# Token-number scatters, first weight loads and two start-up stores in another order (attention, routed experts and a feed-forward layer in one kernel)

## The chip, the cores and the metric

The kernel runs on one core of a Trainium2 chip. The metric is the device time of one execution in microseconds (us). PE is the matmul engine (TensorE) and PEld its weight loads, DVE is VectorE, ACT is ScalarE, POOL is GpSimd, SP is SyncE. SPq, ACTq and POOLq are the instruction queues of those engines as far as they issue transfers (DMAs).

## What is computed

Three layers follow one another. The attention layer pools keys and values by eight, the second layer sends each token to one of eight experts, and the third is a plain feed-forward layer.

```python
k_p = k.reshape(B, H, Sp, 8, D).mean(axis=3)          # q, k, v: (8, 8, 576, 64)
v_p = v.reshape(B, H, Sp, 8, D).mean(axis=3)
attn = softmax(scale * q @ k_p.T)
x = (attn @ v_p) as (4608, 512)                       # one row per token

logits = normed(x) @ normed(expert_emb).T / tau       # 8 experts
expert_idx = argmax(logits); gate_w = softmax(logits)[expert_idx]
for e in range(8):
    h = relu(x[mask_e] @ w1[e])                       # 512 -> 1024
    out[mask_e] = gate_w[mask_e] * (h @ w2[e])        # 1024 -> 512

h = x @ w_in                                          # 512 -> 2048
return (h * clip(h + 3, 0, 6) / 6) @ w_out            # 2048 -> 512
```

## The kernel before

The order of the instructions is written out by hand (a manual schedule): on every engine and queue they run in the order in which the program emits them, and each waits for what it reads or overwrites.

**Phase 1, attention and routing, 36 tiles of 128 tokens.** The loop at line 852 runs over t = 0 to 37. In step t it emits `emit_S(t)` (scores on PE, row maximum and subtraction on DVE), `emit_T(t-1)` (transposes on PE, copy on ACT), the exponential on ACT, the jobs that `todo[t]` holds, `emit_P(t-2)` (attention times values on PE, normalisation on DVE, a store of the tile's rows to `x_dram` from the ACT queue), the jobs of `late[t]`, and at the end of the step at most one entry of the list `prep`. A batch is 4.5 tiles. Its loads (`load_kv`, `load_q`) go out on the SP queue, and its pooling runs on POOL and partly on DVE (`pool_v`, `pool_k0`, `pool_k`; for the first two batches `half_v` and `head_k`). Two buffers of pooled keys, `kps[0]` and `kps[1]`, take turns; both are zeroed on POOL at the start (line 341).

**Routing.** The tiles form six groups of 7, 7, 6, 6, 5 and 5. When a group is through, a generator `emit_route` is put in a list, and `fill` emits a small DVE operation of it at a time between the operations of the tiles. Its last step (lines 571 to 574) writes the token numbers on POOL (`tok`) and then one `scatter` per tile: a tiny memset of `apart` and an indirect DMA of 128 rows of 64 bytes into the table `idx_dram`, each token's number at its place in its expert's list. The table is filled with a dummy number beforehand (lines 759 and 760), and one row of zeros is written behind the tokens of `x_dram` (line 761). Both are issued on the SP queue, the zeros read from `kps[1]`.

**Phase 2, experts, blocks of 256 tokens.** `emit_idx` reads token numbers from the table, `emit_gather` fetches the rows, `emit_wload` fetches a quarter of an expert's w1 or w2 (an indirect DMA from POOL, 512 KB), and `emit_wsplit` splits it into two parts (ACT and POOL or DVE) and emits the load of the same quarter of the next block. Four quarters j make a block: `emit_h(i, j)` needs the split of w1, `emit_y(i, j)` that of w2. In blocks 0 and 1 the w1 split runs on POOL, later on DVE. A block emits w1 splits two quarters ahead and calls `more()` three times per quarter; `more` empties the routing generators little by little. In block 1 at j = 2 all that is left of routing is flushed, and the token lists of the following blocks are asked for.

**The list `prep`** holds what phase 2 needs first: the token lists of three blocks (`ahead`), eight weight loads in one go, the gathers of blocks 0 and 1, the splits of w1 and w2 of quarter 0, the scaling of block 0's rows by their gates (`emit_gated(0)`) and the w1 split of quarter 1. One entry is taken per step from the step in which the expert counts of the first 20 tiles are there; from the third entry on, the gates of those tiles must have been emitted too. If entries are left at t = 36, they are emitted there, before the transposes of block 0 (`emit_xT(0)`).

**Phase 3**, the feed-forward layer, comes behind and isn't touched.

Of the kernel before, what the change touches and what calls it, by code (L numbers as in the profile page):

```python
# [21 lines left out]
def kernel(  # L22
# [27 lines left out]
    NJ = 4  # L50
# [280 lines left out]
    with ExitStack() as p1:  # L331
# [193 lines left out]
        def emit_route(t0, t1):  # L525
# [45 lines left out]
            tok = sm.tile([P, G, IW], I32, name="tok", bufs=2)  # L571
            nc.gpsimd.iota(tok, pattern=[[P, G], [0, IW]], base=P * t0, channel_multiplier=1)
            for t in range(t0, t1):
                scatter(idx_dram, pi[:, t - t0:t - t0 + 1], tok[:, t - t0, :], "ids")
            yield

        def emit_gate(t0, t1):
# [131 lines left out]

        gens = []  # L710

        gates = []
        gate_at = [0]
        calls = [0]
# [37 lines left out]
        for g in range(2):  # L752
# [3 lines left out]
        DR = 18  # L756
        dummy = one.tile([P, DR * IW], I32, name="dummy")
        nc.gpsimd.memset(dummy, NT)
        nc.sync.dma_start(out=idx_dram.rearrange("(p a b) o -> p a (b o)", p=P, b=DR),
                          in_=dummy.unsqueeze(1).to_broadcast([P, IDXN // P // DR, DR * IW]))  # L760
        nc.sync.dma_start(out=x_dram[NT:NT + 1, :], in_=kps[NKP - 1][0:1].rearrange("p h s c -> p (h s c)")[:, 0:XW])
        esq = xp.tile([P, DM], F32, name="sq")
        ess = one.tile([E, 1], F32, name="ess")
        nc.scalar.activation(out=esq[0:E], in_=emb_sb, func=AF.Square, accum_out=ess)
# [61 lines left out]
            at(2, head_k, 1, h, nc.gpsimd if h < HP - 1 else nc.vector, d=late)  # L826
        for g in range(2):
            at(2, half_v, 1, g, nc.gpsimd, d=late)
        at(5, emit_ve1, 1)
        at(6, emit_ve2, 1)  # L830
        for b in range(2, NB):
# [9 lines left out]
        gi = 0  # L841

        prep = [
            lambda: [ahead(i) for i in range(KA)],
            lambda: [emit_wload(w, g) for g in range(NJ) for w in ("w1", "w2")],
            lambda: (emit_gather(0), emit_gather(1)),
            lambda: emit_wsplit("w1", 0, nc.gpsimd),
            lambda: emit_wsplit("w2", 0, nc.gpsimd),
            lambda: emit_gated(0),
            lambda: emit_wsplit("w1", 1, nc.gpsimd),  # L850
        ]
        for t in range(NTILE + 2):
            if t == NTILE:

                while not PRE_U:
                    for g_ in gens + gates:
                        g_[1] = False
                    fill(100)
                if prep:
                    while gates:  # L860
                        for g_ in gens + gates:
                            g_[1] = False
                        fill(100)
                while prep:
                    prep.pop(0)()
                sc = sc_p
                PX[:] = [sc[:, g, :] for g in range(2)]
                emit_xT(0)
            exp = emit_S(t) if t < NTILE else lambda: None
            if 1 <= t <= NTILE:  # L870
                emit_T(t - 1)
            exp()
            for f, *a in todo.get(t, ()):
                f(*a)
            if t == NTILE + 1:
                pt = psA.tile([P, 2, 512], F32, name="pt")
                PY[:] = [pt[:, g, :] for g in range(2)]
                emit_h(0, 0)
            if 2 <= t:
                emit_P(t - 2)  # L880
            for g_ in gens + gates:
                g_[1] = False
            fill(2)
            for f, *a in late.get(t, ()):
                f(*a)
            if gi < len(GROUPS) and t - 2 >= GROUPS[gi][1] - 1:
                gens.append([emit_route(*GROUPS[gi]), False, GROUPS[gi]])
                gi += 1
            if PRE_U and prep and (len(prep) > 5 or not gates):
                prep.pop(0)()  # L890

# [70 lines left out]
    def more():  # L964
        for g_ in gens + gates:
            g_[1] = False
        fill(2)

    def block(i, first):
        key = CONV[i - 1] if 1 <= i <= len(CONV) else None  # L970
        for j in range(NJ):
            g = NJ * i + j
            if i == KA - 2 and j == 2:
                flush(gens)
                flush(gates)
                ahead(KA)
                ahead(KA + 1)
            if j == 0:
# [196 lines left out]
```

## Time and profile before

| | us |
|---|---|
| three runs | 1531.66, 1533.35, 1530.65 (median 1531.66) |
| the profiled execution, whole | 1527.47 |
| its span in the profile | 1525.8 |
| PE busy | 1456.0 (95%) |
| DVE, ACT, POOL busy | 780.3, 626.4, 514.5 |

A share of busy time is a mean over the three phases. Phase 1 takes the first 217 us or so (the transposes of block 0 begin at 217.00 us), the blocks 0 and 1 of phase 2 reach to some 280 us, and from 300 us on PE is busy nearly without a gap. The profiled execution stands 4.2 us under the median of the runs, and 1.7 us of it lie around the span.

### The profile page before, as it was taken

What the parts mean: (1) busy time and instruction counts of PE and PEld (TensorE: products, weight loads), DVE (VectorE), ACT (ScalarE), POOL (GpSimd) and SP (SyncE); (2) the same over time, 40 slices, a digit from 0 to 9 for tenths busy, and PEclk for the clock granted to TensorE, in tenths of its full rate; (3) what the DMA queues carried; (4) which work ended last, traced back from release to release, by engine and by line L of the source; (5) the groups of instructions that cost most, each with busy time, mean ns of one, the idle gap of its engine ahead of it and who ended that gap; (6) DMA issues with size and microseconds to landing.
All of it is one profiled execution on the core that took longest, in us unless ns stands there. A gap on an engine that the chain in (4) does not pass through costs nothing.

```text
span 1525.8 us, 22766 instructions
## 1 busy us (share of the span) xinstructions
PE 1456.0 (95%) x8874; PEld 1304.5 (85%) x8874; DVE 780.3 (51%) x1261; ACT 626.4 (41%) x986; POOL 514.5 (34%) x518
## 2 busy tenths in 40 slices
PE   5889788999999999999999999999999999999997
PEld 4888678899999999999788888888888888888886
DVE  5676646778777777666686322323232222323221
ACT  2545344556556566556343222222222222222221
POOL 3866568665665565545222000010101001010101
PEclk8889789999999999999999999999999999999999
DMA  9765432563862245252322010000101000010000
GB/s 297 259 229 163 163 98 76 169 200 81 266 200 58 75 120 160 72 159 41 113 97 72 0 42 16 29 28 1 56 0 57 1 29 28 5 51 1 28 0 28
DMA packets 88451, 136.15 MB, mean 89 GB/s; under 512 B 43369, under 2 KB 58409, under 8 KB 85874
## 3 DMA queue, kind: packets, MB, share of 16 engines
q1 hardware_dynamic: 45026, 69.10, 14.4%
q0 software_dynamic: 33488, 55.80, 12.2%
q10 hardware_dynamic: 9824, 9.73, 1.9%
q8 instruction: 72, 1.18, 0.3%
q14 instruction: 41, 0.34, 0.1%
HBM read 161.51 MB, written 33.33 MB: 128 GB/s over the span
## 4 chain that ended last, share of the span: by engine, by line
issue 37%; PE 12%; POOL 2%; POOLq 0%; ACT 0%
PE ph L1071 3%; PE psx L1089 3%; PE psy L1071 3%; PE psz L1089 3%; POOL out_dram L128 2%; POOL apart L127 0%; POOLq L1171 0%; POOLq L128 0%; ACT os L1099 0%
## 5 line engine op out<-in xcount | busy, mean ns | idle before, releaser
L157 POOL DMA_INDIRECT rw<-in_w_dram,wrow x179 | 220.1, 1230 | 181.5 <-DVE w1l L170 122.8
L128 POOL DMA_INDIRECT out_dram<-os,idc x36 | 35.1, 976 | 657.8 <-ACT os L1099 651.4
L1075 DVE SCALAR_TENSOR_TENSOR rg<-rg,ph 128x512 f32<-128x512 f32 x72 | 49.6, 689 | 206.9 <-ACT rg L1074 206.9
L1078 DVE TENSOR_TENSOR gl<-rg,gh 128x512 fp32r<-128x512 f32 x144 | 99.8, 693 | 100.7 <-ACT gh L1077 100.7
L1077 ACT ACTIVATE gh<-rg 128x512 fp32r<-128x512 f32 x144 | 91.2, 633 | 145.7 <-DVE rg L1075 144.0
L1075 DVE SCALAR_TENSOR_TENSOR rg<-rg,psy 128x512 f32<-128x512 f32 x72 | 49.5, 687 | 178.3 <-ACT rg L1074 178.3
L1074 ACT ACTIVATE rg<-ph,half 128x512 f32<-128x512 f32 x72 | 49.4, 686 | 208.7 <-PE ph L1071 208.7
L1074 ACT ACTIVATE rg<-psy,half 128x512 f32<-128x512 f32 x72 | 49.4, 686 | 198.7 <-PE psy L1071 198.7
L277 PE MATMUL psy<-hh,w2h 128*128 128x256 f32 x640 | 129.4, 283 | 0.0
L277 PE MATMUL psy<-hh,w2l 128*128 128x256 f32 x640 | 127.5, 280 | 0.0
L277 PE MATMUL psy<-hl,w2h 128*128 128x256 f32 x640 | 127.4, 280 | 0.0
L170 DVE TENSOR_TENSOR w1l<-rw,w1h 128x1024 fp32r<-128x1024 f32 x76 | 108.9, 1433 | 24.9 <-ACT w1h L169 14.9
L170 DVE TENSOR_TENSOR w2l<-rw,w2h 128x1024 fp32r<-128x1024 f32 x84 | 108.6, 1293 | 15.9 <-ACT w2h L169 11.8
L1089 PE MATMUL psx<-wol,gh 128*128 128x512 f32 x288 | 112.0, 389 | 0.0
L1089 PE MATMUL psz<-woh,gh 128*128 128x512 f32 x288 | 112.0, 389 | 0.0
L1089 PE MATMUL psx<-woh,gh 128*128 128x512 f32 x288 | 112.0, 389 | 0.0
L1089 PE MATMUL psx<-woh,gl 128*128 128x512 f32 x288 | 112.0, 389 | 0.0
L1089 PE MATMUL psz<-wol,gh 128*128 128x512 f32 x288 | 112.0, 389 | 0.0
L1089 PE MATMUL psz<-woh,gl 128*128 128x512 f32 x288 | 112.0, 389 | 0.0
L265 ACT ACTIVATE hh<-ph 128x512 fp32r<-128x512 f32 x78 | 46.6, 598 | 147.0 <-PE ph L262 135.9
L169 ACT ACTIVATE w2h<-rw 128x1024 fp32r<-128x1024 f32 x85 | 89.9, 1058 | 29.5 <-PE psy L277 18.5
L262 PE MATMUL ph<-xh,w1h 128*128 128x256 f32 x624 | 99.0, 280 | 1.5 <-ACT xh L248 1.5
(235 smaller groups left out, 3340.0 us busy)
## 6 DMA issues: line engine op xcount, KB each, us to landing
yT_dram<-ys SPq DMA_DIRECT2D x21, 512.0 KB
x_dram<-x ACTq DMA_DIRECT2D x36, 256.0 KB
raw<-in_w_in_dram SPq DMA_DIRECT2D x16, 512.0 KB
raw<-in_w_out_dram SPq DMA_DIRECT2D x16, 512.0 KB
yl<-yT_dram SPq DMA_DIRECT2D x8, 1024.0 KB
k_t<-in_k_dram SPq DMA_DIRECT2D x7, 1152.0 KB
q_t<-in_q_dram SPq DMA_DIRECT2D x7, 1152.0 KB
v_t<-in_v_dram SPq DMA_DIRECT2D x7, 1152.0 KB
```

The lines of the kernel that those rows point to most:

```text
L128: ins = nc.gpsimd.indirect_dma_start(out=dst, out_offset=bass.IndirectOffsetOnAxis(ap=idx, axis=0), in_=src, in_offset=None)
L157: nc.gpsimd.indirect_dma_start(out=RAW[nm][j], out_offset=None, in_=WROWS[nm], in_offset=bass.IndirectOffsetOnAxis(ap=wrow[:, i, j:j + 1], ...
L169: nc.scalar.activation(out=h, in_=r, func=AF.Copy)
L170: eng.tensor_tensor(out=l, in0=r, in1=h.bitcast(F32), op=ALU.subtract)
L262: nc.tensor.matmul(ph[:, f, :], lhsT=a[:, c, fs], rhs=b[:, c, :], start=(n == 0), stop=(n == 3 * KD - 1))
L277: nc.tensor.matmul(o, lhsT=a[:, f, P * c:P * c + P], rhs=b[:, f, :], start=(j == 0 and n == 0 and c % 2 == 0), stop=(j == NJ - 1 and n == ...
L1071: nc.tensor.matmul(ph, lhsT=a[:, c, :], rhs=b[:, c, :], start=(n == 0), stop=(n == 3 * KD - 1))
L1074: nc.scalar.activation(out=r, in_=ph, func=AF.Relu, scale=1.0 / 6.0, bias=half)
L1075: nc.vector.scalar_tensor_tensor(out=r, in0=r, scalar=1.0, in1=ph, op0=ALU.min, op1=ALU.mult)
L1077: nc.scalar.activation(out=gh, in_=r, func=AF.Copy)
L1078: nc.vector.tensor_tensor(out=gl, in0=r, in1=gh.bitcast(F32), op=ALU.subtract)
L1089: nc.tensor.matmul(PO[a], lhsT=x[:, ts], rhs=w, start=(f == 0 and n == 0), stop=(f == NF - 1 and n == 2))
```

## The change

- The scatters of a group are no longer emitted in one go: they go into a list `pend`, and `put(n)` emits n of them. A step of phase 1 that takes no entry of `prep` puts one, or two if more than seven wait. In phase 2 each `more()` puts one. All that wait are put before the first `ahead` and at the flush in block 1.
- `prep` has eight entries instead of seven: the eight weight loads of block 0 are spread over entries 2, 3, 5, 6, 7 and 8 (two, two, one, one, one, one), the gathers come fourth.
- The dummy fill of the table is emitted with the jobs of t = 3, behind the loads of batch 2 (t = 1); it stays on the SP queue.
- The row of zeros is issued on the ACT queue, at its old place in the program, where the first ACT operation of the kernel (square of the expert embeddings, line 764) now comes behind it.

```diff
-                scatter(idx_dram, pi[:, t - t0:t - t0 + 1], tok[:, t - t0, :], "ids")
+                pend.append(lambda t=t: scatter(idx_dram, pi[:, t - t0:t - t0 + 1], tok[:, t - t0, :], "ids"))
             yield
...
+        pend = []
+
+        def put(n=1):
+            while pend and n > 0:
+                n -= 1
+                pend.pop(0)()
...
-        nc.sync.dma_start(out=idx_dram.rearrange("(p a b) o -> p a (b o)", p=P, b=DR),
-                          in_=dummy.unsqueeze(1).to_broadcast([P, IDXN // P // DR, DR * IW]))
-        nc.sync.dma_start(out=x_dram[NT:NT + 1, :], in_=kps[NKP - 1][0:1].rearrange("p h s c -> p (h s c)")[:, 0:XW])
+
+        def fill_idx():
+            nc.sync.dma_start(out=idx_dram.rearrange("(p a b) o -> p a (b o)", p=P, b=DR),
+                              in_=dummy.unsqueeze(1).to_broadcast([P, IDXN // P // DR, DR * IW]))
+
+        nc.scalar.dma_start(out=x_dram[NT:NT + 1, :], in_=kps[NKP - 1][0:1].rearrange("p h s c -> p (h s c)")[:, 0:XW])
...
+        at(3, fill_idx)
...
-            lambda: [ahead(i) for i in range(KA)],
-            lambda: [emit_wload(w, g) for g in range(NJ) for w in ("w1", "w2")],
+            lambda: (put(99), [ahead(i) for i in range(KA)]),
+            lambda: (emit_wload("w1", 0), emit_wload("w2", 0)),
+            lambda: (emit_wload("w1", 1), emit_wload("w2", 1)),
             lambda: (emit_gather(0), emit_gather(1)),
-            lambda: emit_wsplit("w1", 0, nc.gpsimd),
-            lambda: emit_wsplit("w2", 0, nc.gpsimd),
-            lambda: emit_gated(0),
-            lambda: emit_wsplit("w1", 1, nc.gpsimd),
+            lambda: (emit_wsplit("w1", 0, nc.gpsimd), emit_wload("w1", 2)),
+            lambda: (emit_wsplit("w2", 0, nc.gpsimd), emit_wload("w2", 2)),
+            lambda: (emit_gated(0), emit_wload("w1", 3)),
+            lambda: (emit_wsplit("w1", 1, nc.gpsimd), emit_wload("w2", 3)),
         ]
...
             if PRE_U and prep and (len(prep) > 5 or not gates):
                 prep.pop(0)()
+            else:
+                put(1 + (len(pend) > 7))
...
         fill(2)
+        put()
...
                 flush(gates)
+                put(99)
                 ahead(KA)
```

## Rows read from the trace of the kernel before

**Rows 1.** Stretches: length, busy us and instructions of PE, PEld, DVE, ACT, POOL; clock, DMA.
```profile
7.00:217.00 210.00, 168.41 (x1175) 155.63 (x1176) 133.18 (x396) 94.94 (x207) 130.65 (x148) 0.85 0.65 211
217.00:300.00 83.00, 73.88 (x581) 70.76 (x580) 56.17 (x107) 40.43 (x60) 64.76 (x57) 0.96 0.32 96
300.00:990.00 690.00, 687.98 (x4806) 643.00 (x4805) 434.90 (x515) 344.37 (x491) 285.15 (x233) 1.00 0.35 103
```

**Rows 2.** Timeline, 13 to 41 us: start, duration, operation, [idle before it, its releaser].
```profile
13.84 14.53 SPq L761 DMA_DIRECT2D x_dram<-kp  x1
...
30.06 0.35 ACTq L491 DMA_DIRECT2D x_dram<-x  x1
...
35.25 0.51 DVE L789 TENSOR_TENSOR kp<-k_t 64x72 f32<-64x72 f32 x2 [4.35 <-DMA x_dram<-kp]
...
37.47 1.63 PE L434 MATMUL sc<-kp,q_t 128*64 128x144 f32 x10 [4.51 <-DVE ex L445]
...
40.71 1.22 PE L434 MATMUL sc<-kp,q_t 128*64 128x144 f32 x6 [1.61 <-POOL kp L789]
```

**Rows 3.** Timeline of the first 20 us.
```profile
3.99 1.09 POOL L341 MEMSET kp<- 128x576 f32 x2
...
6.08 0.46 DVE L785 TENSOR_TENSOR k_t<-k_t 128x288 f32<-128x288 f32 x1 [1.02 <-DMA k_t<-in_k_dram]
...
19.82 0.44 PE L394 MATMUL pm<-ident,vs 96*64 96x96 f32 x3 [2.01 <-POOL vs L780]
```

**Rows 4.** Timeline, 201 to 210 us: the fourth group's scatters.
```profile
201.52 1.01 POOL L128 DMA_INDIRECT idx_dram<-tok,pi  x1 [0.25 <-issue]
...
207.62 0.17 DVE L476 TENSOR_SCALAR rd<-px 128x8 f32<-128x8 f32 x1 [6.81 <-remote]
...
207.96 0.97 POOL L128 DMA_INDIRECT idx_dram<-tok,pi  x1 [0.21 <-issue]
...
209.17 3.26 PE L468 MATMUL px<-vp,eT 96*128 96x146 f32 x12 [5.35 <-DVE oh L543]
```

**Rows 5.** One stretch inside that series, columns as in Rows 1.
```profile
204.00:208.00 4.00, 0.00 (x0) 0.00 (x0) 0.38 (x4) 0.00 (x0) 3.22 (x7) 1.00 0.04 6
```

**Rows 6.** PE's waits, 0 to 226 us: us in total, times, longest.
```profile
PE pt L455 <- ACT ex L449: 5.1, 3, 2.4
```

**Rows 7.** Groups of instructions, 0 to 330 us: count, busy us, mean ns, idle before.
```profile
L157 POOL DMA_INDIRECT rw<-in_w_dram,wrow x41 | 48.4, 1179 | 30.1 <-DVE SH L586 10.7 <-DVE w1l L170 8.2 <-issue 6.1
L128 POOL DMA_INDIRECT idx_dram<-tok,pi x36 | 35.4, 982 | 31.8 <-DVE LG L487 17.5 <-issue 9.1 <-DVE x L484 4.9
L170 POOL TENSOR_TENSOR w1l<-rw,w1h 128x1024 fp32r<-128x1024 f32 x10 | 23.9, 2391 | 6.1 <-ACT w1h L169 5.9
```

**Rows 8.** Timeline around the end of phase 1 and in blocks 0 and 1.
```profile
214.45 1.32 ACT L234 ACTIVATE xg<-xg 128x512 f32<-128x512 f32 x2
...
217.00 1.04 PE L244 MATMUL sc<-ident,xg 128*128 128x128 f32 x8
...
218.86 0.63 ACT L490 ACTIVATE sq<-x 128x512 f32<-128x512 f32 x1 [1.77 <-DVE x L484]
...
219.49 1.04 ACT L169 ACTIVATE w1h<-rw 128x1024 fp32r<-128x1024 f32 x1
...
225.17 2.38 POOL L170 TENSOR_TENSOR w1l<-rw,w1h 128x1024 fp32r<-128x1024 f32 x1
...
254.33 2.36 POOL L170 TENSOR_TENSOR w1l<-rw,w1h 128x1024 fp32r<-128x1024 f32 x1
...
256.75 1.22 PE L262 MATMUL pm<-xh,w1l 128*128 128x256 f32 x4 [3.59 <-POOL w1l L170]
```

**Rows 9.** Timeline: one DVE addition beside a POOL addition, and one alone.
```profile
59.07 3.45 POOL L376 TENSOR_TENSOR v_t<-v_t 96x1536 f32<-96x1536 f32 x1
...
60.07 2.76 DVE L362 TENSOR_TENSOR k_t<-k_t 128x288 f32<-128x288 f32 x1
...
82.53 0.45 DVE L362 TENSOR_TENSOR k_t<-k_t 128x288 f32<-128x288 f32 x1
```

## The prediction

> **What bounds the kernel now.** I read the stretches first. From 300 to 990 us PE is busy 687.98 of 690 us at full clock [rows 1], so nothing that the change touches can shorten anything there: whatever it gains or loses must show before 300 us and is then carried to the end unchanged. Between 7 and 217 us PE is busy 168.4 of 210 us, idle for 41.6, at a mean granted clock of 0.85; between 217 and 300 it is idle for 9.1 [rows 1]. No engine is full there (DVE 133, ACT 95, POOL 131 us of 210), so phase 1 is a chain of waits between engines. The clock adds to each wait: 168.4 us at 0.85 would be 143.1 at 1.0, so 25.3 us are lost to the lower clock beside 41.6 us of idling, 0.6 us for each idle us. I use 1.6 as the price of an idle us in phase 1; it is a mean, and the first us of the kernel have their part in it.
>
> Then I looked for the idle time in the timeline and found two kinds that the change touches. **One is the row of zeros.** SP needs 14.53 us to issue it, behind the fill of the table [rows 2]. It reads `kps[1]`, so the writes of batch 1's pooled keys wait for it: DVE until 35.25, idle for 4.35, and through DVE PE until 37.47, idle for 4.51; POOL, late by the same wait, holds PE for another 1.61 at 40.71 [rows 2]. **The other is less plain.** While the six scatters of the fourth group run on POOL, from 201.52 to 208.9, DVE stands idle for 6.81 us before it reads matmuls that were finished before 204, and PE for 5.35 behind it [rows 4]. In the four us from 204 PE and ACT do nothing, DVE 0.38 us, the DMA engines are at 0.04, and POOL alone is busy [rows 5]. So no data is missing, and no bandwidth. PE's three waits for the exponential, 5.1 us in all [rows 6], lie in, or within three us behind, one of the first three series. I take it that signals between engines arrive late while POOL issues indirect DMAs one behind another; the trace shows the coincidence, not the cause.
>
> **The change part by part.**
>
> *Row of zeros to ACT, fill behind batch 2's loads.* The row no longer stands behind the fill. It can go when POOL has zeroed `kps[1]`, at 5.08 [rows 3], and the ACT queue issues a store in 0.35 us [rows 2]; nothing shows its landing, but it has over 25 us before DVE wants `kps[1]`. Both waits of PE go: 4.51 + 1.61 = 6.12 us, with the clock 9.8. Late next are the additions on DVE themselves, which end just when PE has run out of work. Two costs stand against it. The embeddings' square on ACT now waits until about 5.4, where it could start without this store, and the ten DVE operations of the embedding norm behind it come before the first pooling of keys, which starts at 6.08 [rows 3]: up to 2.3 us of delay for the first scores. PE stands idle for 2.01 us at 19.82 for the pooled values, whose loads are not touched [rows 3], so I count nothing, and at most 0.3 if that cover is too short. The fill itself now goes past the loads of batch 2, and behind it on SP stand the queries of batch 2 and all of batch 3. If SP is held for 14.53 us again, those loads leave later; before, batch 2's loads stood there. I count nothing and price it as a rival.
>
> *Scatters one or two a step.* 36 indirect DMAs of 0.98 us [rows 7] stay; none is saved. From the first scatter of [rows 4] to the sixth it is 6.44 us, so 1.29 us each with the memset. Groups 1 to 3 now go out singly between t = 12 and 29 (the last three before the first token lists). The idle time that I put down to the series is 5.35 + 5.1 = 10.45 us [rows 4, 6], with the clock 16.7. The ends are far apart: nothing, if the coincidence misleads, and (41.6 - 6.1) x 1.6 = 57 if all other idling of phase 1 hung on it [rows 1, 2]. I take 16.7, what those rows show.
>
> *Weight loads two a step.* Eight loads of 1.18 us [rows 7] become 2 + 2 and then single ones. The same bytes go out, earlier than phase 2 reads them. Their gain is of the same kind as the scatters', no row prices it, and I count nothing: between zero and another 5.35 us as at [rows 4], which the upper end above contains.
>
> *What is moved into phase 2.* From t = 29 to 35 every step takes an entry of `prep`, and then `put` isn't called. So the fourth group (six scatters) and the fifth (five) wait until t = 36; four go there and at t = 37, and the rest one per `more()`, together with the sixth group's five. All of them now stand on POOL between the w1 splits of blocks 0 and 1, and there POOL is the bound: PE waits 3.59 us at 256.75 for the split that POOL begins at 254.33 [rows 8], and POOL is busy 64.8 of 83 us [rows 1]. In order of emission: behind the w1 split of quarter 1 and before that of quarter 5 there stood five scatters; now there are 14 (four at t = 36 and 37, three in each of the quarters 0 to 2, one in quarter 3). That is 9 x 1.29 = 11.6 us more, and one weight load (w2, quarter 3) with its gap, 1.3 us. Against it, the split of quarter 1 can begin earlier. It stood behind the fifth group's scatters until 225.17; now only ACT holds it, with the square at 218.86 (0.63, and about 0.2 for reading the sum), the scaling of block 0 (1.32) and the split's first half (1.04), to about 222.1 [rows 8]: 3.0 us less. Sum +9.9 us at the wait of 256.75. Behind it two scatters are left, which the next splits can bear. The ends are 3 us (if PE finds other work) and (11 x 1.29 + 1.3) x 1.6 = 25, with every moved scatter and the clock.
>
> *`prep` is one step longer.* The scaling of block 0's rows moves from t = 34 to the end of t = 35, and PE's transposes, which begin at 217.00 without a wait, come after it: ACT reaches it only behind the square at 218.86 [rows 8], so PE stands idle for some 3.3 us, and block 0 begins 1.6 to 3 us later. This lies ahead of the POOL chain, which makes PE wait anyway; I count nothing beyond the 9.9. Without that cover it costs up to 3.3 x 1.6 = 5.3.
>
> **Sum:** -9.8 - 16.7 + 9.9 = -16.6 us. Against the profiled 1527.5 that is 1510.9. The median stands 4.2 us above that execution, so 1515.
>
> **The rivals.** About 0.2%, 3 us, is what a measurement of this kernel can tell from no change.
>
> *The series aren't the cause.* Idle time moves from one place to the next and only the zero row pays: -9.8 + 9.9 = 0, 1532. For it: a coincidence that repeats is no proof, and the releaser is named "remote" [rows 4]. Against: in [rows 5] nothing else runs.
>
> *Slower: POOL's chain in blocks 0 and 1.* As above, but PE also runs at the lower clock behind each of its waits, 9.9 x 1.6 = 15.8: -9.8 + 15.8 = +6, 1538. It decides as soon as the split of quarter 5 ends over 6 us later against the end of phase 1 and phase 1 itself gains no more than the zero row. For it: 3.59 us of such a wait exist already [rows 8]. Against: it needs the whole second term to be nothing.
>
> *The fill keeps SP shut where it now stands.* Queries of batch 2 or keys of batch 3 come late, and DVE and PE wait for them as they did for the zero row. At the price of that wait the first term is given back: -6.8, 1525. This is also the case that the change doesn't do at the start what it says.
>
> *DVE's additions meet POOL's.* The addition of two halves of the keys on DVE takes 0.45 us alone and 2.76 us when it starts while POOL is in an addition of 3.45 us: it ends with POOL's [rows 9]. With the scatters out of the way POOL comes to these additions at other times. If that happens once more in three batches, 3 x 2.31 x 1.6 = 11 us are lost: 1526. By the Trainium skill, "SBUF — State Buffer", section "Who interferes with whom", a VectorE operation with two SBUF inputs contends with a GpSimd operation that reads SBUF, and the one that comes second is blocked for the whole of the other. The trace agrees in the pair of rows 9, and the rule speaks against packing POOL's additions more densely; scatters don't read such operands, so it gives them no such cost.
>
> *More than forecast.* POOL finds room in phase 2, or the unlisted gaps go too: under 1498.
>
> **How the numbers follow.** Forecast 1515 with a chance of 0.53 (own range 1500 to 1527, which is a second term of 32 and of 5 us); more than forecast 0.08; additions 0.10; fill 0.06; no gain from the series 0.12; slower 0.11. Faster by over 0.2%: 0.53 + 0.08 + 0.10 + 0.06 = 0.77; within 0.2%: 0.12; slower: 0.11. The range of 1498 to 1534 leaves out the first of the rare cases below (0.08) and the slower one above (0.11).
>
> **What would show it.** Right: DVE's write of batch 1's pooled keys no longer waits for `x_dram<-kp`; the scores of the fifth tile begin some 4 us earlier; no stretch of 4 us like [rows 5] in phase 1; the transposes of block 0 begin 20 us or more earlier than 217.00; and between them and the h of block 1's quarter 1 PE loses about 10 us to POOL's w1 splits. Wrong: stalls of the same length beside single scatters or loads (then the series were not the cause), or PE waits for w1 splits over 15 us in all. A third wrong outcome would be a wait on loads between 30 and 60 us.

## The result and the profile after

The changed kernel takes 1511.13 us (median of 4 runs, 1509.30 to 1517.08) against 1531.16 us for the kernel before measured beside it: a ratio of 0.9881, 95% interval 0.9843 to 0.9919, so 12 to 24 us or 18 us in the middle. The profiled execution took 1510.78 us, with a span of 1509.1 against 1525.8 before.

First the stretches of the kernel after, with the columns of [rows 1]; phase 1 ends some 27 us earlier, and the second stretch has the same 83 us.

```profile
7.00:190.00 183.00, 151.55 (x1179) 141.15 (x1180) 145.94 (x411) 94.25 (x209) 121.13 (x131) 0.93 0.72 233
190.00:273.00 83.00, 67.59 (x495) 63.79 (x494) 51.05 (x98) 36.33 (x54) 68.36 (x67) 0.92 0.29 85
300.00:990.00 690.00, 687.52 (x4737) 639.19 (x4736) 422.11 (x510) 337.82 (x484) 276.80 (x232) 1.00 0.32 97
```

In phase 1 PE is idle for 183 - 151.55 = 31.4 us instead of 41.6, at a clock of 0.93 instead of 0.85. In the 83 us behind it PE is idle for 15.4 us instead of 9.1. From 300 us PE is as full as before.

The next fence groups the transposes of a gathered block (line 244): operation, tile, count; ns shortest/median/longest; first and last start. `sc` are blocks 0 and 1, `psx` begins with block 2.

```profile
L244 PE MATMUL psx<-ident,xg x160: 270/272/329, 257.1 to 706.2; 128*128 128x128 f32 x160
L244 PE MATMUL sc<-ident,xg x16: 271/272/273, 189.6 to 221.7; 128*128 128x128 f32 x16
...
L244 PE MATMUL psx<-ident,xg x160: 270/272/328, 274.4 to 722.5; 128*128 128x128 f32 x160
```

The last line is the kernel before. Block 0's transposes start at 189.6 instead of 217.0 [rows 8]: phase 1 gained 27.4 us. Block 2's start at 257.1; before it was 274.4, so 17.3 us are left, and 10.1 us were given back in blocks 0 and 1. These two starts give three lengths for every run below: phase 1, the start of phase 2 (before 57.4 us, after 67.5), and the rest (span minus the second start: before 1251.4, after 1252.0). Each comes from one execution, and several of the profiled executions lie off the median of their runs: the kernel before 4.2 us below, `e1_zero` 3.8 above, `e2_series` 3.8 below, `e9_oldzero` 3.7 above, `e10_dve` 5.3 below. A difference of a few us between two traces is therefore not yet one of the kernels.

Where it came back, in PE's waits from 190 to 300 us (us in total, times, longest):

```profile
PE pm L262 <- POOL w1l L170: 5.0, 3, 2.9
PE ph L262 <- POOL w1l L170: 3.4, 1, 3.4
PE psx L244 <- ACT xg L234: 2.6, 2, 2.4
PE pt L277 <- issue: 2.5, 4, 1.1
```

PE waits 8.4 us for POOL's w1 splits; before it was 3.9 us in the same place (3.59 of them in [rows 8]).

The start of the kernel after, and the place where the zero row had held DVE [rows 2, 3]:

```profile
5.31 0.48 ACTq L771 DMA_DIRECT2D x_dram<-kp  x1
5.83 1.28 ACT L774 ACT_TABLE_LOAD   x1 [5.83 <-POOL dummy L765]
7.13 0.63 ACT L774 ACTIVATE sq<-emb_sb 8x512 f32<-8x512 f32 x1
...
10.16 0.44 DVE L795 TENSOR_TENSOR k_t<-k_t 128x288 f32<-128x288 f32 x1
...
11.62 0.82 PE L434 MATMUL sc<-kp,q_t 128*128 128x144 f32 x2 [11.62 <-DVE kp L799]
...
29.87 0.99 DVE L796 TENSOR_TENSOR k_t<-k_t 128x144 f32<-128x144 f32 x1
30.95 2.26 DVE L799 TENSOR_TENSOR kp<-k_t 64x72 f32<-64x72 f32 x2
31.32 1.80 POOL L788 TENSOR_TENSOR v_t<-v_t 96x768 f32<-96x768 f32 x1
34.92 1.46 PE L434 MATMUL sc<-kp,q_t 128*64 128x144 f32 x9 [3.82 <-DVE ex L445]
```

The store holds back not only the square on ACT but also the load of its table behind it, so the first scores start at 11.62 instead of 7.57. DVE no longer waits for `x_dram<-kp` (35.25 before), but its two writes of `kp` take 2.26 us together instead of 0.51, beside POOL's additions; the fifth tile's scores come at 34.92 instead of 37.47.

The fill of the table goes out at 21.37, behind the loads of batch 2, and the loads of batch 3 stand behind it on SP (the values at 38.07). POOL waits for these values:

```profile
20.00:38.00 18.00, 13.79 (x100) 12.69 (x100) 13.89 (x26) 7.81 (x18) 14.88 (x18) 0.87 1.02 298
38.00:56.00 18.00, 17.47 (x140) 16.80 (x139) 13.93 (x34) 10.38 (x23) 8.24 (x9) 0.94 0.95 330
...
55.80 3.49 POOL L376 TENSOR_TENSOR v_t<-v_t 96x1536 f32<-96x1536 f32 x1 [9.01 <-DMA v_t<-in_v_dram]
```

PE waits for no load there. Up to then the DMA engines are full (1.02 and 0.95 in these stretches), as they were before (1.06 and 0.92).

One piece of the old stall is still there. Two weight loads, four scatters, two gathers and a fifth scatter form a new row on POOL from 195.8 to 207.5 us, in phase 2:

```profile
205.15 0.28 PE L277 MATMUL pt<-hl,w2h 128*128 128x256 f32 x1 [1.14 <-issue]
205.88 0.28 PE L277 MATMUL pt<-hl,w2h 128*128 128x256 f32 x1 [0.45 <-issue]
206.49 1.00 POOL L128 DMA_INDIRECT idx_dram<-tok,pi  x1 [0.22 <-issue]
207.51 2.38 POOL L170 TENSOR_TENSOR w1l<-rw,w1h 128x1024 fp32r<-128x1024 f32 x1
208.90 0.60 ACT L265 ACTIVATE hh<-pm 128x512 fp32r<-128x512 f32 x1 [4.81 <-remote]
```

ACT reads at 208.90 a product that PE had finished by 202.4 and stands idle for 4.81 us, as DVE did in [rows 4]; PE issues one matmul in 0.7 us meanwhile. For these matmuls the view names no wait at all (`issue`), so late signals don't account for PE's own slowness there, and no run shows what does.

### The profile page after: what moved, and what is told of

The parts are those of the page before. It is cut to its first block, busy times and chain, and to the rows that moved or that the text cites. A ratio compares the mean times of both kernels' runs of the same rounds, so it can differ in the third digit from the quotient of the medians.

```text
span 1509.1 us, 22766 instructions
## 1 busy us (share of the span) xinstructions
PE 1442.2 (96%) x8874; PEld 1291.6 (86%) x8874; DVE 786.9 (52%) x1261; ACT 625.7 (41%) x986; POOL 514.2 (34%) x518
## 4 chain that ended last, share of the span: by engine, by line
issue 38%; PE 7%; DVE 3%; POOL 2%; ACT 1%; POOLq 0%; ACTq 0%; DVEq 0%
POOL out_dram L128 2%; PE ph L1087 2%; PE psx L1105 2%; PE psz L1105 2%; PE psy L1087 2%; DVE cva L939 1%; DVE rg L1091 1%; DVE cva L941 1%; DVE gl L1094 1%; ACT gh L1093 1%; DVE cva L940 0%; DVE yl L959 0%; POOL apart L127 0%; DVE cva L942 0%; POOL wol L951 0%
## 5 line engine op out<-in xcount | busy, mean ns | idle before, releaser
L157 POOL DMA_INDIRECT rw<-in_w_dram,wrow x179 | 214.1, 1196 | 177.0 <-DVE w1l L170 125.5
L170 DVE TENSOR_TENSOR w1l<-rw,w1h 128x1024 fp32r<-128x1024 f32 x76 | 102.7, 1351 | 26.4 <-ACT w1h L169 13.9
L169 ACT ACTIVATE w2h<-rw 128x1024 fp32r<-128x1024 f32 x85 | 89.9, 1057 | 31.3 <-PE psy L277 20.6
L262 PE MATMUL ph<-xh,w1l 128*128 128x256 f32 x624 | 98.7, 280 | 3.4 <-POOL w1l L170 3.4
```

Of the source, the lines that this page charges most:

```text
L157: nc.gpsimd.indirect_dma_start(out=RAW[nm][j], out_offset=None, in_=WROWS[nm], in_offset=bass.IndirectOffsetOnAxis(ap=wrow[:, i, j:j + 1], ...
L169: nc.scalar.activation(out=h, in_=r, func=AF.Copy)
L170: eng.tensor_tensor(out=l, in0=r, in1=h.bitcast(F32), op=ALU.subtract)
L262: nc.tensor.matmul(ph[:, f, :], lhsT=a[:, c, fs], rhs=b[:, c, :], start=(n == 0), stop=(n == 3 * KD - 1))
```

## The experiments

A run's time is given with the kernel before that was measured beside it. The first eight runs, on two chips, stood beside a kernel before of 1529.2 and 1530.8 us. The last four (`e9_oldzero` to `e12_all`) ran on two other chips of the same kind, where the kernel before takes 1518.4 us. The changed kernel itself was timed only for the result above, beside 1531.16 us, so the first eight are set against it by their ratios, and its interval of 0.9843 to 0.9919 goes into each such difference. The last four are compared only with one another.

**The zero row alone.** The kernel before, with the store on ACT and the fill behind batch 2's loads:

```diff
-        nc.sync.dma_start(out=idx_dram.rearrange("(p a b) o -> p a (b o)", p=P, b=DR), ...)
-        nc.sync.dma_start(out=x_dram[NT:NT + 1, :], in_=kps[NKP - 1][0:1]...)
+        nc.scalar.dma_start(out=x_dram[NT:NT + 1, :], in_=kps[NKP - 1][0:1]...)
...
+        at(3, fill_idx)
```

> The kernel before with the zero row's store moved to ACT and the fill to t = 3, nothing else. By the sum of the prediction 9.8 us less than before: about 1521. The trace of the changed kernel shows two things against that: the first scores start at 11.62 instead of 7.57, and the pooled keys of batch 1 on DVE take 2.26 instead of 0.51 us beside POOL's additions; its sixth tile is 4.6 us ahead. So the theory of a half-lost first term says 4.6 x 1.0 to 1.6, 1524 to 1527. If the row of zeros paid nothing at all: 1531.

Measured: 1525.06 us, ratio 0.9981 (0.9965 to 0.9998), that is 3 us, or 0.3 to 5.4. At the 14th tile's scores it is 2.4 us ahead of the kernel before (78.67 against 81.07), at the end of phase 1 1.1 us behind (218.1 against 217.0). PE's waits up to there, columns as above:

```profile
PE px L468 <- DVE oh L543: 8.1, 1, 8.1
PE pt L455 <- ACT ex L449: 5.8, 3, 2.8
```

Before these were 5.3 and 5.1 us [rows 4, 6]. So in this execution the lead was lost inside the series of scatters. Alone, the first term is worth a third of its 9.8 us.

How large the lead is at the 14th tile, though, isn't settled by the series. `e2_series`, the next run, emits the same instructions up to there, on the same chip. Its first scatter goes out at 73.7 us, and its 14th tile's scores begin at 73.79, 7.3 us ahead of the kernel before instead of 2.4. The two traces part where DVE's addition of keys meets POOL's of 3.4 us in one and not in the other (here, then `e2_series`):

```profile
56.24 3.22 DVE L362 TENSOR_TENSOR k_t<-k_t 128x288 f32<-128x288 f32 x1
...
61.09 2.26 PE L434 MATMUL sc<-kp,q_t 128*128 128x144 f32 x8 [3.07 <-issue]
...
55.76 0.45 DVE L362 TENSOR_TENSOR k_t<-k_t 128x288 f32<-128x288 f32 x1
...
57.84 1.22 PE L434 MATMUL sc<-kp,q_t 128*128 128x144 f32 x8 [0.29 <-issue]
```

**The scatters back in series.** The changed kernel with one line undone:

```diff
-                pend.append(lambda t=t: scatter(idx_dram, ...))
+                scatter(idx_dram, ...)
```

> The changed kernel, but every group's token-number scatters go out in one series again. Theory that series make signals late: the stalls of the first four series come back, ACT and DVE idle 2 to 7 us in each, phase 1 (start of block 0's transposes) ends 10 to 17 us later than in the changed kernel, and blocks 0 and 1 gain some of it back; 1516 to 1523 in all. Rival, series aren't the cause: phase 1 ends where it does in the changed kernel (189.6), and without the scatters on POOL's chain in blocks 0 and 1 the time is 1501 to 1505.

Measured: 1522.80 us, ratio 0.9972 (0.9956 to 0.9988), that is 0.0091 or 14 us worse than the changed kernel (8 to 20 us with both intervals). Block transposes and PE's waits of phase 1:

```profile
L244 PE MATMUL psx<-ident,xg x160: 270/272/476, 264.5 to 713.7; 128*128 128x128 f32 x160
L244 PE MATMUL sc<-ident,xg x16: 270/272/274, 204.2 to 232.9; 128*128 128x128 f32 x16
...
PE pt L455 <- ACT ex L449: 5.8, 3, 2.8
PE px L468 <- DVE x L484: 4.9, 5, 2.3
PE px L468 <- DVE oh L543: 4.2, 1, 4.2
```

Phase 1 ends 14.6 us later than in the changed kernel, with the stalls of [rows 4, 6] back; the start of phase 2 takes 264.5 - 204.2 = 60.3 us, 7.2 less. The rival by which the series cost nothing is out on this chip, where it was run: it wanted phase 1 at 189.6 and 1501 to 1505.

**The weight loads back in series.** The eight loads in one step, the scatters still spread:

```diff
-            lambda: (emit_wload("w1", 0), emit_wload("w2", 0)),
-            lambda: (emit_wload("w1", 1), emit_wload("w2", 1)),
+            lambda: [emit_wload(w, g) for g in range(NJ) for w in ("w1", "w2")],
```

> The changed kernel with its eight first weight loads in one series again (and one step of the preparation less); the scatters stay spread. Series theory: a stall of 3 to 5 us in phase 1 behind the series, as before at 185 to 188 us; but the loads no longer stand among the scatters that go out between 195 and 207 us, so at most 5 us in all: 1509 to 1516. If only scatters make signals late, or loads are harmless: phase 1 unchanged, 1506 to 1511.

Measured: 1513.56 us, ratio 0.9908 (0.9887 to 0.9929). Phase 1 ends at 191.6, 2.0 us later; the intervals overlap. The loads' part in the time is at most small, though signals come late beside them too: four rises of PE's semaphore stand at 167.4 to 167.6 us, right behind the row of eight loads (155.9 to 166.0) and some 4 us behind the last end of a matmul (how they are counted: see below).

**Scatters also in the steps of the preparation.** `put` in every step, so that fewer scatters are left for phase 2:

```diff
                 prep.pop(0)()
-            else:
-                put(1 + (len(pend) > 7))
+            put(1 + (len(pend) > 7))
```

> The changed kernel, but scatters also go out one a tile in the steps that work off the preparation. In the changed kernel four scatters, two gathers and two weight loads meet between 195.8 and 207.5 us; ACT starts on a finished matmul 4.81 us late there, and PE waits 8.4 us for w1 splits on POOL. Theory (POOL's chain with 9 scatters too many, and a new series): that stall and most of the waits go, block 1 begins 8 to 10 us earlier: 1501 to 1504. Rival, POOL's time is only moved ahead of the splits of the last tiles: 1509 to 1513.

Measured: 1506.69 us, ratio 0.9871 (0.9847 to 0.9896). Phase 1 ends at 183.5, 6.1 us earlier, but block 1 began only 2.0 us earlier (219.7 against 221.7 for its last transpose); block 2 began 7.0 us earlier, at 250.1. There is one longer wait in block 0:

```profile
207.94 1.22 PE L262 MATMUL pm<-xh,w1l 128*128 128x256 f32 x4 [7.86 <-POOL w1l L170]
```

POOL issues nine indirect DMAs from 192.9 to 205.5 ahead of that split. The row moved with the scatters, and both forecasts, 1501 to 1504 and 1509 to 1513, were missed. The ratio's interval overlaps the changed kernel's.

**The store behind the square.** The changed kernel with the two lines on ACT exchanged:

```diff
-        nc.scalar.dma_start(out=x_dram[NT:NT + 1, :], ...)
         nc.scalar.activation(out=esq[0:E], in_=emb_sb, func=AF.Square, accum_out=ess)
+        nc.scalar.dma_start(out=x_dram[NT:NT + 1, :], ...)
```

> The changed kernel with the zero row's store behind the square of the embeddings on ACT instead of ahead of it. The first scores start at 7.6 again instead of 11.6. Theory that the wait for the pooled values at 20 to 26 us covers the start: the scores of the fifth tile move by less than 1 us, total 1509 to 1511. Rival, the 4 us at the start count in full: 1505 to 1507.

Measured: 1511.82 us, ratio 0.9870 (0.9848 to 0.9892). First scores at 7.53. The fifth tile's came at 29.98, 4.9 us earlier, which neither expectation had; the sixth waited 3.88 us for DVE and came at 37.42, 3.3 us ahead, and phase 1 ended at 190.4, 0.8 us later than in the changed kernel. The 4 us at the start cost nothing in the end. The trace shows what takes the lead:

```profile
31.21 8.50 SPq L358 DMA_DIRECT2D q_t<-in_q_dram  x1
...
34.51 1.32 DVE L362 TENSOR_TENSOR k_t<-k_t 128x288 f32<-128x288 f32 x1 [3.25 <-DMA k_t<-in_k_dram]
```

DVE, for which the sixth tile waits, itself waits for the keys of batch 2. And the load of queries right behind the fill takes 8.50 us to issue, as the zero row behind it had taken 14.53 [rows 2]; in the changed kernel it comes due at 37.13 and takes 0.34.

**Three scatters a step.** `put(3)` instead of `put(1 + (len(pend) > 7))`.

> The changed kernel, but three scatters go out a step while any wait, instead of one or two. If the harm grows with the length of a series: some 2 to 4 us of phase 1 are lost against the changed kernel, 1513 to 1516. If only long series (six, seven) hurt: phase 1 as in the changed kernel, 1509 to 1512. If any three in a row hurt as much as seven: 1520 and more.

Measured: 1512.34 us, ratio 0.9876 (0.9854 to 0.9898), phase 1 to 191.1. Rows of three aren't told from single scatters.

**The series with other work in between.** `e2_series` with four small memsets ahead of each scatter:

```diff
+    space = const.tile([1, 240], F32, name="space")
...
         nc.gpsimd.memset(apart, 0.0)
+        for _ in range(4 if group == "ids" else 0):
+            nc.gpsimd.memset(space, 0.0)
```

> The kernel with the scatters in series again (e2_series, 1522.8), with about 1.2 us of other work on POOL ahead of each of these scatters, so that a series takes twice as long and half as many indirect DMAs go out per us. If signals are late because indirect DMAs go out densely: the stalls of phase 1 shrink although POOL is busier, phase 1 ends before e2_series' 204.2, total 1512 to 1519. If they are late because POOL is held for a long stretch, whatever it does: the stalls grow, phase 1 ends later than 204.2, total 1526 to 1535.

Measured: 1553.98 us, ratio 1.0157 (1.0133 to 1.0181): slower than either theory gave. Which waits PE had tells more than the time. First two scatters of the first group, then PE's largest waits up to the end of phase 1 (lines are three further down in this kernel):

```profile
74.59 1.14 POOL L131 DMA_INDIRECT idx_dram<-tok,pi  x1 [2.88 <-DVE pi L573]
...
77.26 0.97 POOL L131 DMA_INDIRECT idx_dram<-tok,pi  x1 [0.17 <-issue]
...
PE sc L437 <- POOL kp L373: 14.4, 2, 11.5
PE sc L437 <- DVE kp L802: 12.4, 2, 11.9
PE sc L437 <- DVE ex L448: 7.8, 5, 3.6
PE px L471 <- DVE x L487: 7.7, 4, 2.9
...
L247 PE MATMUL sc<-ident,xg x16: 270/272/273, 199.0 to 250.5; 128*128 128x128 f32 x16
```

With scatters 2.5 to 2.7 us apart, PE's waits for the exponential (5.8 us in `e2_series`) and for `oh` (4.2) are gone, and phase 1 ends at 199.0 instead of 204.2, although it now holds an ordinary wait of 11.5 us (`e2_series`' trace lies 3.8 us below its median, this one at it): the second group's scatters run from 111.9 to 127.9, and the next batch's pooled keys stand behind them on POOL. In phase 2 the ordinary waits win: PE waits 32.9 us for w1 splits that stand behind spaced scatters. So two things were mixed in "the series": signals that are late while the DMAs go out 1.3 us apart, and work that stands behind them on POOL.

**Both, and no scatter in the last two steps.** `e4_putall` with the exchange of `e5_start` and `if t < NTILE:` ahead of `put`.

> e4_putall (1506.7) with the store behind the square as in e5_start, and without scatters in the two steps behind the last tile. In e4_putall nine indirect DMAs still stand in a row from 192.9 to 205.5 us there, and PE, DVE and ACT are idle together for 2.19 and 3.30 us in that stretch. Theory: these 5.5 us go: 1499 to 1503. Rival, the scatters only crowd later steps and the stall moves there: 1505 to 1508.

Measured: 1507.82 us, ratio 0.9862 (0.9838 to 0.9886), phase 1 to 184.8, start of phase 2 67.6 us. No gain over `e4_putall`; the rival that the stall only moves was right: PE, DVE and ACT are idle together for 2.89 us at 201.5.

**The zero row where it was.** The changed kernel without its first part.

> The changed kernel with the zero row and the fill where they stood before: scatters and weight loads spread, nothing else. DVE waits for x_dram<-kp at 35.25 again. If the two parts add up (the zero row alone brought 3 us in e1_zero): 1514. If the zero row is worth more once the series no longer swallow its gain (the 9.8 of the prediction): 1521. If later waits swallow it here too: 1511.

Measured: 1509.50 us, ratio 0.9944 (0.9928 to 0.9961) against a kernel before of 1518.44. That it lies below 1511 says nothing, since the chip is another; the expectations can't be decided by the time. The trace can be set beside the next run's, from the same chip, whose code up to phase 2 differs only in the zero row and the fill. The scores of the 14th tile, first here, then there:

```profile
80.88 1.22 PE L434 MATMUL sc<-kp,q_t 128*64 128x144 f32 x16
...
73.83 1.22 PE L434 MATMUL sc<-kp,q_t 128*64 128x144 f32 x16
```

That is 7.05 us, and 13.6 at the end of phase 1 (193.4 against 179.8). Neither is the price of the zero row. Here too a meeting of DVE's addition with POOL's stands in between (2.72 us at 59.91, against 0.46 in the other trace), and the two traces lie 3.7 us above and 5.3 below the medians of their runs. By the times, `e11_pool4` below, from the same chip, is faster by some 4 us (0.9919 against 0.9944; 0.3 to 7 us with both intervals), and it differs from this run in the zero row, the fill and one head of batch 1. So with the scatters spread the zero row shows about what it brought alone, and not 9.8 us.

**The w1 splits of blocks 0 and 1 on DVE.**

```diff
-            emit_wsplit("w1", g + 2, nc.gpsimd if i < KA - 1 else nc.vector)
+            emit_wsplit("w1", g + 2)
```

> The changed kernel, but the w1 splits of blocks 0 and 1 on DVE instead of POOL (those of the preparation stay). Theory that POOL's chain of scatters, loads and splits bounds the start of phase 2: PE's 8.4 us of waits for w1l on POOL go, and what replaces them on DVE is under 3 us: 1503 to 1507. Rival, the stall in the row of indirect DMAs at 196 to 208 us bounds it, not the splits: that stays, 1509 to 1512.

Measured: 1485.28 us, ratio 0.9790 (0.9773 to 0.9807). The transposes, then the stretch from 180 to 240 us here and in the changed kernel (columns as in [rows 1]):

```profile
L244 PE MATMUL psx<-ident,xg x160: 270/272/330, 228.0 to 674.8; 128*128 128x128 f32 x160
L244 PE MATMUL sc<-ident,xg x16: 270/272/273, 179.8 to 204.7; 128*128 128x128 f32 x16
...
180.00:240.00 60.00, 56.95 (x473) 55.00 (x472) 45.91 (x105) 35.48 (x53) 50.17 (x58) 1.00 0.37 113
...
180.00:240.00 60.00, 48.90 (x361) 45.92 (x360) 31.34 (x77) 27.78 (x44) 51.08 (x55) 0.91 0.35 116
```

The start of phase 2 takes 48.2 us; in `e9_oldzero` and `e11_pool4`, on the same chip and with the splits on POOL, it takes 67.3 and 69.9. No wait of PE for a split is left. That is about 20 us, more than the 8.4 us of waits that PE shows: behind each wait stood a lower clock (0.91 against 1.00 in these stretches; 0.89 in `e11_pool4`) and further waits. By the times it is 20.6 us against `e11_pool4`. From 186.4 to 237.7 POOL issues 34 indirect DMAs in a row, and no signal of PE, ACT or DVE is late (counted below): the row alone doesn't make signals late on this chip.

**Batch 1's fourth head on POOL.** `nc.gpsimd` for all heads of batch 1.

> The changed kernel, but the fourth head of batch 1's keys is added on POOL too, where POOL waits 1.72 us at 26 for its values, instead of on DVE beside POOL's additions (3.77 us there instead of 1.27). Theory that DVE's additions beside POOL's gave back the zero row's gain: the scores of the fifth tile begin at 31 to 32 instead of 34.92, total 1505 to 1508. Rival, the next wait takes it: 1510 to 1512.

Measured: 1505.91 us, ratio 0.9919 (0.9903 to 0.9935). The fifth tile's scores begin at 30.58, a little earlier than expected, since POOL finishes these keys in the time in which it had waited. Against `e10_dve` from the same chip phase 1 is no shorter (182.6 against 179.8), so by the end of phase 1 the lead was spent. Part of it goes as in `e5_start`: DVE waits 1.50 us for the keys of batch 2 at 33.63, the sixth tile's scores wait 2.65 at 36.74, and the load behind the fill takes 6.89 us to issue.

**Three of these edits together.** `e4_putall`, `e10_dve` and `e11_pool4` together.

> The changed kernel with the three edits that helped: scatters also in the steps of the preparation (e4_putall), batch 1's fourth head on POOL (e11_pool4), w1 splits of blocks 0 and 1 on DVE (e10_dve). e10_dve is at 0.979 of the kernel before measured beside it; e4_putall and e11_pool4 brought 4 to 5 us each in phase 1. If the three add up: 0.972 to 0.975; if the scatters' place no longer matters once POOL splits nothing in blocks 0 and 1: 0.976 to 0.979. The trace also tells two readings of e10_dve apart, in which 34 indirect DMAs stood in a row without one signal more than 1.5 us late: if it was the chip, which showed none in the two runs beside it either, late signals (1.5 us and more) may be seen here in the row behind 185 us; if the missing POOL split ended them, none here, on any chip.

Measured: 1484.18 us, ratio 0.9787 (0.9768 to 0.9805), the same as `e10_dve` alone. Neither the place of the scatters nor the fourth head shows a gain once POOL splits nothing in blocks 0 and 1. On late signals it settles nothing: this chip too shows none.

**Late signals, counted.** The trace records when a semaphore rises. First counted are completions of PE, ACT and DVE (12 to 1520 us, some 2,900 a run) for which the next rise of the engine's semaphore is recorded over 1.5 us after the instruction's end ("next rise"). That mixes two things, because in the first ten kernels 180 to 222 of the rises aren't recorded at all, and the next one is then another instruction's. In the changed kernel ACT's exponential that ended at 131.04 counts as 7.25 us late, but PE's transposes, which wait for it, began at 133.19. So the last two columns count only rises that no instruction of the engine ended within 1.5 us before: these are late.

```
kernel        next rise   not recorded   late, phase 1   late, to 1000 us
before            99           193             10               13
after             89           204              0                4
e1_zero           75           186             12               15
e2_series        105           180              8               12
e3_wloads         79           201              4                8
e4_putall         68           189              1                7
e5_start          95           201              0                4
e6_three          95           215              2                4
e7_spaced         73           197              0                2
e8_both           89           222              1                7
e9_oldzero         0             0              0                0
e10_dve            0             0              0                0
e11_pool4          1             0              0                0
e12_all            0             0              0                0
```

All the late rises are PE's. In phase 1 they stand in the kernels with rows of scatters or loads, and spreading or spacing the scatters takes them away but for two at most, and for four where the loads stand in a row (`e3_wloads`). In [rows 4] PE's last operation of that stretch ended at 203.8 and its semaphore's next rise stands at 207.60, 0.02 us ahead of DVE's start. In the four runs on the other chips no rise is late and none is missing, whatever the kernel. Each chip was used in one stretch of time, so chip and hour aren't separated; and no kernel with the scatters of phase 1 in series was traced on the other chips.

## Why the prediction was right, and where it was wrong

**The sum** was -16.6 us and the span fell by 16.7. Step by step: phase 1 was to gain 9.8 + 16.7 = 26.5 and gained 27.4. Blocks 0 and 1 were to give back 9.9 and gave back 10.1. The rest changed by 0.6. The median of 1511 lies 4 below the forecast of 1515, which had added the distance of the first median from the profiled execution. That the sums agree to 0.1 us is partly luck. Both spans are single executions, and the parts measured singly don't add up to the 27.4 us of phase 1: some 3 for the zero row, 14.6 for the series and 2.0 for the loads are 19.6. What gained the other 8 us no run shows, and the scatter of single executions is of that size.

**POOL's chain** is the best step, right in place, kind and size: 14 scatters were foretold between the splits of quarters 1 and 5, 13 stand there, and the two splits lie 41.8 us apart (193.18 to 234.96) instead of 29.2 [rows 8], where 12.9 more were foretold. `e10_dve` shows what it hid. I counted only the scatters that the change moves there. The chain had cost the kernel before 57.4 - 48.2 = 9.2 us already, worked out across two chips. The slower rival, the chain paid with the lower clock, had its mechanism: the clock was 0.92 in the 83 us behind phase 1, against 0.96 before [rows 1]. But 10.1 us came back and not its 15.8, and its condition, that phase 1 gain nothing else, didn't come.

**The series** term, 16.7, was close to what undoing that part alone costs phase 1, 14.6 (`e2_series`). The rival that the series aren't the cause is out on the chip of `e2_series`; that the chip of the first result is of the same sort is argued from its late rises (13 before, 4 after). But the reason I gave, signals late while POOL issues indirect DMAs one behind another, is half of one. As far as the rises on record show, only PE's signals are late, so PE's own waits for the exponential would have come second hand, through ACT and DVE. `e7_spaced` shows that distance ends the lateness in phase 1, and `e10_dve` and the count show that on other chips a row of 34 makes none. The chip (or the hour) is a second condition that no row of one trace could show. What it is stays open. On such a chip the changed kernel without its zero row still is 0.56% faster than the kernel before, so something of the spreading is left; how much is the plain order on POOL wasn't separated.

**The zero row**, 9.8, was mis-sized, and its share of the sum came right by luck. Alone it brought 3 us (`e1_zero`), and with the scatters spread some 4 (0.3 to 7) together with one head (`e9_oldzero` against `e11_pool4`). The waits of [rows 2] did go. But the step that each idle us is worth 1.6, whatever follows, doesn't hold there, for two reasons that the traces show. The DMA engines are full up to 56 us, so batches 2 and 3 come when their loads land; the mean share of 0.65 in [rows 1] hid that, and "a chain of waits between engines" is not true of this part. And whether DVE's addition meets POOL's at 56 to 62 us decides over another 3 us of PE's idling, and did so differently in two executions of the same instructions.

**The start** was mis-sized. I had the square wait until 5.4 and missed the load of ACT's table, 1.28 us, which stands behind the store in the order; the delay was 4.05 us, not at most 2.3. That I counted it at nothing was right, as `e5_start` shows, but not for the reason given alone: the pooled values cover it only in part, and the rest went in the sixth tile's wait for the keys of batch 2.

**DVE's additions beside POOL's**, a rival with 0.10, did come. The additions of line 362 on DVE up to 220 us, first before and then after (columns as in [rows 7]):

```profile
L362 DVE TENSOR_TENSOR k_t<-k_t 128x288 f32<-128x288 f32 x12 | 10.1, 842 | 1.2 <-POOL k_t L786 1.2
...
L362 DVE TENSOR_TENSOR k_t<-k_t 128x288 f32<-128x288 f32 x12 | 15.3, 1272 | 0.0
```

Their mean rose from 842 to 1272 ns, and the pooled keys of batch 1 took 1.75 us more. By the Trainium skill, "SBUF — State Buffer", section "Who interferes with whom", a VectorE operation with two SBUF inputs contends with a GpSimd operation that reads SBUF. The trace agrees. What it cost in all isn't shown. `e11_pool4` takes the first case away, starts the fifth tile 4.3 us earlier than the changed kernel (on another chip) and has no shorter phase 1 than its neighbour; but later cases stay. PE's longest wait between 40 us and the end of phase 1, 3.61 us, follows two DVE operations of the routing that ended with POOL's additions, and that take 0.20 and 0.17 us alone:

```profile
132.29 2.74 DVE L564 TENSOR_TENSOR rr<-rr,oh 128x48 f32<-128x48 f32 x1
...
135.32 1.55 DVE L570 CAST pi<-po 128x6 int32<-128x6 f32 x1
...
137.61 1.84 PE L468 MATMUL px<-vp,eT 96*128 96x146 f32 x12 [3.61 <-DVE x L484]
```

Another wait of PE, 2.75 us at 118.04, follows an addition of line 362 that took 3.72 us at 112.74.

**The longer `prep`**, up to 3.3 us of idling at block 0's transposes, wasn't there: they begin at 189.56 without a wait, because ACT reaches the scaling at 188.18.

**The fill**, a rival with 0.06, came in part. SP is shut behind it again, up to 8.50 us (`e5_start`), but in the changed kernel the next load comes due only when SP is free. POOL waits 9.01 us for batch 3's values, and neither DVE nor PE waits for a load there, so the first term wasn't given back by it. How much of POOL's wait is the fill and how much the full DMA engines wasn't separated.

**Signs.** Right were DVE's lost wait, the transposes over 20 us earlier, no stretch like [rows 5] in phase 1, and some 10 us lost in blocks 0 and 1. Wrong was "the fifth tile some 4 us earlier" (2.6; the sixth has 4.6). Of the signs against me, the stall of 4.81 us at 208.90 belongs to a row of nine and not to single scatters. The third, a wait on loads between 30 and 60 us, came, on POOL.

## What to carry to other kernels

When work is taken out of one place on an engine's queue, find where it lands and count what stands behind it there: here 10 of 27 us came back through eight more scatters and a weight load ahead of a split, and moving the splits off that engine, on top of the change, was worth 20 us more. Measure each of several edits alone and taken away from the whole, and by the times of many runs: two single traces put the zero row at 13.6 us where the times say 3 to 4. Look at the share of the DMA engines stretch by stretch before a wait is called one between engines. A stall that no data, no bandwidth and no busy engine explains may depend on the chip; look at a second one before the kernel is shaped around it. And before a rise of a semaphore is called late, count whether all rises are recorded.

## What the runs showed of the hardware

I had not expected chips of one kind to differ in this. On some a completed matmul's signal rises late, by 6.50 us behind a matmul that ended at 202.4 in the changed kernel, while POOL issues indirect DMAs 1.3 us apart, and 6 to 8% of all rises are missing from the trace; on others no signal was late and none missing, in 48 us and more of such a row. The kernel before is 12 us faster on the latter, near the 10.45 us of idling that I had put down to the series [rows 4, 6]; no trace of it was taken there, so that these are the same us isn't shown. Spacing the scatters to 2.5 us took away PE's waits for the exponential and for `oh`, and with them every late rise of phase 1 (`e7_spaced`: none, `e2_series`: eight).
